# GpSimd adds the last shifted array of VectorE's key tiles, a bank at a time beside VectorE's reads of PSUM

## The chip, the cores and the metric

The kernel runs on one core of a Trainium2 chip. The metric is the device time of one launch in microseconds (us), the median of several runs. A core has TensorE (matmuls, PE in the profile), VectorE (DVE), ScalarE (ACT), GpSimd (POOL) and SyncE (SP, which here only issues DMAs). A profile is one separate execution with the hardware profiler on; its span runs from the first to the last recorded instruction.

## What is computed

An attention block and a gated feed-forward block over the same 2048 rows of 512, mixed by a gate per row. The feed-forward block takes `A_x` too.

```python
def _A_ref(x, wqkv, wo):                       # 32 heads of 16
    q, k, v = ...                              # (x @ wqkv), split by head
    scores = einsum("bhqd,bhkd->bhqk", q, k) * (Dh ** -0.5)
    p = softmax(scores, axis=-1)
    return einsum("bhqk,bhkd->bhqd", p, v)... @ wo

def _B_ref(x, w_gate, w_up, w_down):           # hidden size 1792
    return (silu(x @ w_gate) * (x @ w_up)) @ w_down

g = sigmoid((x * gate_w).sum(-1, keepdims=True))
return g * _A_ref(...) + (1 - g) * _B_ref(...)
```

## The kernel before

**Units and key tiles.** Attention is cut into 32 units: a block of 512 queries by a group of 4 heads. A unit has 16 key tiles of 128 keys, so there are 512 key tiles in all. A key tile has four banks of scores, one for each head: 128 keys by 512 queries in fp32, one PSUM bank each. For every tile TensorE makes the scores, some engine makes exponentials of them, and TensorE multiplies these by V into the unit's accumulator `o_ps` (a "P·V pass": four matmuls, one for each head, in four column strips of the array).

**Two ways to an exponential.** Most tiles go through ScalarE: a score group of two banks (`s_t`) is read by one activation that writes two banks of bf16 to `e_all`. The others go through VectorE, which builds bf16 bit patterns: an eviction of each bank `d_t` (`first`, inside `emit_d`, line 845) multiplies by EXP_A, adds EXP_B and writes uint16 into the tile's array `y` of 4 x 512 columns. Read as bf16 this is a rough exponential. Such a tile is finished in one of two ways:

- four arrays: `copy` (line 887) adds the constants 25, 56 and 94 (`SHIFTS`) to the whole array, each into an array of its own; TensorE does four P·V passes, on `y` and on the three shifted arrays, whose errors cancel out in the sum. This costs VectorE four evictions and three additions of 128 x 2048.
- two arrays: `bits` (line 895) masks the array twice and `product` (line 904) multiplies; TensorE does two P·V passes. VectorE does four evictions, two masks and one product.

`quad` (line 1542) chooses between the two by how much time TensorE has to spare in the plan.

**Arrays.** The arrays (`c_t`, in seven slots, NS; the last slot lies in `kaug` or `wd_t`) are taken by `take_home` and given back by `drop` when their last reader is planned to end. At most three tiles have a live `y` (NY, counted by `y_live`).

**The plan.** The order on every engine is fixed while the kernel is built. A planner keeps clocks for TensorE, ScalarE and VectorE (`plan.pe`, `plan.act`, `plan.dve`) and adds a price in microseconds for each instruction that it emits; `ordered` ties each instruction behind the one before it on its engine. Work for VectorE waits in three lists:

- `owed`: evictions and small steps of projections, the feed-forward block and the normalisation, put there by `later` with a price and the time at which it may start, and emitted by `pay`;
- `d_wait`: evictions of `d_t` (`pay_d`);
- `vops`: the additions, masks and products over whole arrays (`pay_v`).

`fill_dve` (line 924) takes from these by an order of preference as long as VectorE's clock is behind TensorE's. `v_unit` (line 1517) decides whether a further key tile goes to VectorE: it does if VectorE, by its clock and its queued work, can be done before ScalarE ends the tiles it still has. So the share of the two engines follows from the prices. `force` (line 384) emits a chain of work at once when something needs it.

**Feed-forward and projections.** They run as column matmuls between the score groups, paced by deadlines (`Pacer`). Their results are read from PSUM by VectorE and, for the gate's tanh, by ScalarE.

**GpSimd** only fills constants at the start. All DMAs are on SP's and ScalarE's queues.

Of the kernel before, what the change touches and what calls it, by code (L numbers as in the profile page):

```python
# [11 lines left out]
BF16 = mybir.dt.bfloat16  # L12
F32 = mybir.dt.float32
U16 = mybir.dt.uint16
F16 = mybir.dt.float16


# [62 lines left out]
def kernel(  # L80
# [99 lines left out]
            return lambda *a, **kw: ordered(f(*a, **kw))  # L180

    vec = Ordered(nc.vector)
    queue = Ordered(nc.sync)


# [95 lines left out]
    for j in range(4):  # L281
        nc.gpsimd.memset(sel_t[32 * j:32 * j + 1, j:j + 1], 1.0)

    kb = const.tile([P, NB], F32, name="kb")
    gval = const.tile([P, KT], F32, name="gval")
    omg = const.tile([P, KT], F32, name="omg")
# [4 lines left out]


    class Plan:
        pe = dve = act = 0.0
        mode = last = None
        seq = 0
        slot = -1
# [13 lines left out]
    FLIP, UNIT_US = 0.105, 0.217  # L311
    TO_ACT, ACT_FIX, ACT_COL, ACT_IN = 0.485, 0.064, 0.4265, 0.167
    ACT_PE, DVE_PE, PE_DVE, ACT_DVE = 0.055, 0.08, 0.24, 0.06

    def spend(mode, mms, ready=0.0):

# [2 lines left out]
        plan.pe = max(plan.pe + (FLIP if mode != plan.mode else 0.0), ready) + (0.226 if mode == "F" else UNIT_US) * mms  # L319
        plan.mode = mode  # L320

    def later(cost, f, ready=None, key=None):

        c = plan.chain
        if c is not None:
            c.owed += 1
        ready = plan.pe + PE_DVE if ready is None else ready
        owed.insert(sum(o[0] <= ready for o in owed), (ready, cost, f, c, key))

    def spend_v(cost, ready=0.0, key=None):  # L330

        if key is not None and key == plan.last:
            cost += 0.13
        plan.last = key
        plan.dve = max(plan.dve, ready) + cost

    def pay(i=0):
        ready, cost, f, c, key = owed.pop(i)
        spend_v(cost, ready, key)
        keep, plan.chain = plan.chain, None  # L340
        f()
        plan.chain = keep
        if c is not None:
            c.owed -= 1
            if c.done():
                c.done_at = plan.slot
# [35 lines left out]
        return mms  # L382

    def force(c):
        for a in c.after + c.begun:
            force(a)
        while not c.out():
            while c.cond is not None and not c.cond():
                if owed:
                    pay()  # L390
                else:
                    for f in at.pop(min(at)):
                        f()
            emit_piece(c)
        while c.owed:
            pay()
# [135 lines left out]
    def q_pieces(qb, b):  # L532
        def landed(p):
            me = plan.chain
            later(0.6, lambda: end(p, me), key=("q", b))

        def rows(t, r):
            for hh in range(8):
                gg, j = hh // 4, hh % 4
                if (b, gg) != (0, 0):  # L540
                    queue.dma_start(out=get_q(qb, 2 * b + gg)[32 * j + r:32 * j + r + DH, j % 2, :],
                                      in_=t[DH * hh:DH * (hh + 1), :])

        def end(p, me):
            qst = work.tile([P, QBW], BF16, tag="qst", name="qst")
            vec.tensor_copy(out=qst[:, :], in_=p[:, :])
            m_free(p, plan.dve)
            rows(qst, 0)

            aq = work.tile([P, QBW], BF16, tag="aq", name="aq")  # L550

            def mag():
                vec.tensor_scalar(out=aq[:, :].bitcast(U16), in0=qst[:, :].bitcast(U16), scalar1=0x8000, scalar2=None,
                                  op0=ALU.bitwise_or)
                plan.chain = me
                later(0.21, weigh, plan.dve, ("q", b))

            def weigh():
                vec.tensor_scalar(out=aq[:, :], in0=aq[:, :], scalar1=kb[:, b:b + 1], scalar2=None, op0=ALU.mult)
                rows(aq, DH)  # L560
            plan.chain = me
            later(0.21, mag, plan.dve, ("q", b))
        return columns(DC, "qp", lambda dc: wqk[:, dc, P * b:P * (b + 1)],
                       lambda dc: xT[:, dc, qb * QBW:(qb + 1) * QBW], landed)

    def q0_pieces(qb):

        st = {}

        def landed(p):  # L570
            st["p"] = p
            later(0.6, mag, key=("aq", qb))
            later(0.21, clear, key=("aq", qb))

        def mag():
            vec.tensor_copy(out=mt[:, 5, :], in_=st["p"][:, :])

        def clear():
            vec.tensor_scalar(out=mt[:, 5, :].bitcast(U16), in0=mt[:, 5, :].bitcast(U16), scalar1=0x7FFF, scalar2=None,
                              op0=ALU.bitwise_and)  # L580

        def bound():
            bound_add(st["p"], kneg0, mt[:, 5, :])
            spend("C", 1)
            variants(st["p"], q0[qb], work.tile([P, QBW], BF16, tag="qst", name="qst")[:, :])
        return (columns(DC, "qp", lambda dc: wpad[0][:, dc, :], lambda dc: xT[:, dc, qb * QBW:(qb + 1) * QBW], landed),
                [(1, bound, False)])
# [6 lines left out]
    def variants(p, to, q, more=()):  # L594
# [7 lines left out]
                vec.tensor_scalar(out=to[:, v, :], in0=q, scalar1=vsel[:, v:v + 1], scalar2=None, op0=ALU.mult)  # L602
        key = object()
        later(0.6, copy, key=key)
        later(0.4, select, key=key)
        for cost, f in more:
            later(cost, f, key=key)

    def gate_end():
# [3 lines left out]
        def end():  # L613
# [1 line left out]
            vec.reciprocal(gval[:, :], omg[:, :])  # L615
            vec.tensor_tensor(out=omg[:, :], in0=ge[:, :], in1=gval[:, :], op=ALU.mult)
            vec.reciprocal(odds[:, :], ge[:, :])
        later(0.5, end, plan.act + ACT_DVE)

    def turn_odds():  # L620
        rd = work.tile([P, QBW], BF16, tag="rd", name="rd")[:, :].bitcast(F32)
# [223 lines left out]
    def emit_d(i, rows=32):  # L845
# [12 lines left out]
        def first():  # L858
# [4 lines left out]
                              op0=ALU.mult, op1=ALU.add)  # L863
            m_free(d_t, plan.dve)
            cur[0] -= 1
            if cur[0]:
                return
            plan.last = ("y", n)
            if groups[n] == 2:
                vops.extend([(0.6, lambda: bits(n, 0, y), ("y", n), n, True), (0.6, lambda: bits(n, 1, y), None, n, True),  # L870
                             (MUL_US, lambda: product(n, h, y), None, n, False)])
            else:
                users[h][0] = 2
                ready(n, 0, h, y)
                for k in range(1, 4):
                    vops.append((0.6, lambda k=k: copy(n, k, h, y), ("y", n) if k == 1 else None, n, True))
        d_wait.append((plan.pe + UNIT_US + PE_DVE, first, n))

    waiting = {}
    copies = {}  # L880
# [6 lines left out]
    def copy(n, k, i, y):  # L887
        h, c = home()
        vec.tensor_scalar(out=c, in0=y, scalar1=SHIFTS[k - 1], scalar2=None, op0=ALU.add)
        ready(n, k, h, c)  # L890
        if k == 3:
            drop(i, plan.dve + 0.05)
            y_live[0] -= 1

    def bits(n, k, y):
        h, c = home()
# [21 lines left out]

    def pay_v():
        cost, f, key, _, _ = vops.pop(0)  # L920
        spend_v(cost, 0.0, key)
        f()

    def fill_dve():

        while plan.dve <= plan.pe + 0.2:
            now = plan.dve
            due = [k for k, o in enumerate(owed) if o[0] <= now + 0.05]
            free = [k for k in due if owed[k][4] is None or owed[k][4] != plan.last]
            fit = bool(vops) and vops[0][3] // KT <= closed + AHEAD and c_ready() <= now  # L930
            if fit and vops[0][3] // KT < au and vops[0][2] != plan.last:
                pay_v()
            elif d_wait and d_wait[0][2] // KT < au and d_wait[0][0] <= now + 0.05:
                pay_d()
            elif free:
                pay(free[0])
            elif d_wait and d_wait[0][0] <= now + 0.05:
                pay_d()
            elif fit and vops[0][2] != plan.last:
                pay_v()  # L940
# [1 line left out]
                pay(due[0])  # L942
            elif fit:
                pay_v()
            elif d_wait or owed or vops and vops[0][3] // KT <= closed + AHEAD:
                t = min([w[0] for w in d_wait] + [o[0] for o in owed[:1]]
                        + [c_ready()] * bool(vops and vops[0][3] // KT <= closed + AHEAD))
# [108 lines left out]
    def recip(qb, g1, n0):  # L1056
# [9 lines left out]
        def spread():  # L1066
# [8 lines left out]
            for b in range(g1 // 2):  # L1075
                queue.dma_start(out=rb[:, b, :],
                                  in_=rr[8 * b:8 * b + 8, :].unsqueeze(1).broadcast_to([8, DH, QBW]))
        at.setdefault(n0 + 6, []).append(lambda: later(1.1 if full else 0.87, spread))
        for b in range(g1 // 2):
            def norm(b=b):  # L1080
                vec.tensor_tensor(out=onc[qb][:, b, :], in0=onc[qb][:, b, :], in1=rb[:, b, :], op=ALU.mult)
                normed.add((qb, b))
            at.setdefault(n0 + 13 + b, []).append(lambda norm=norm: later(0.345, norm))

    def denominators(p, osb):
        for tq in range(TQ):
# [140 lines left out]
    def bound_all():  # L1227
        def f():
            k_neg(kneg0, 1, kneg1)
            k_neg(kneg0, 2, kneg0)  # L1230
        later(0.8, f)

    def q0_again(p):

# [5 lines left out]
            plan.act += 0.48  # L1240
            ratio_done.append(0)
        variants(p, q0[0], q0_bf[1])
        at.setdefault(8, []).append(lambda: later(0.6, differ))
        at.setdefault(10, []).append(scale)

    def scale_part(p):
# [16 lines left out]
    q_of[0] = again  # L1263

    def gate_column():
        later(0.1, lambda: vec.tensor_copy(out=wv[:, :, 63:64], in_=gw_col[:].unsqueeze(2)))
    gate_w_in = pace.add([(0.2, gate_column, False)], 9, 11, [v_late])
    v_rest = [pace.add(v_pieces(tt), 2, int(14 + 3 * tt), [gate_w_in]) for tt in range(KT)]

# [14 lines left out]
    for qb in range(QB):  # L1284
        for b in range(NB):
            d = UNIT.index((qb, max(2 * b, 1))) * KT
            after = []
            if qb == 0:
# [3 lines left out]
                    ks += prev  # L1292

                def bnd(b=b):
                    later(2.46, lambda: k_bound(b))
                after = prev = [pace.add([(0.2, bnd, False)], 0, d - 34, ks)]

            if b == 0:
# [191 lines left out]
    def next_pv():  # L1490
        flush_act()
        while not pv_list(None):
# [3 lines left out]
                pay_v()  # L1496
            elif owed:
                pay()
            else:
                lone_d()  # L1500
        emit_pv(pv_list(None)[0])
# [15 lines left out]
    def v_unit():  # L1517
# [4 lines left out]
        while vu < UNITS:  # L1522
            if vu > au + 1 or vu in q_of and not (q_of[vu].done() and (vu < QB or plan.slot >= q_of[vu].done_at + 3)):
                return None
            left = hi[vu] - (at_ + begun if vu == au else 0)
            if vu >= au and left > 0 and (vu or hi[0] > KT // 2):
                end = plan.act + (left - 1) * TILE_US + ((hi[au] - at_) * TILE_US if vu > au else 0.0)
                busy = sum(v[0] for v in vops) + 0.6 * (len(owed) + len(d_wait))
# [78 lines left out]
                continue  # L1607
        emit_group(w, ride, rel)
    flush_act()
    while closed < UNITS or vops or vcur:  # L1610
        fill_dve()
        while owed and owed[0][0] <= plan.pe:
            pay()
# [86 lines left out]
```

## Time and profile before

| what | us |
|---|---|
| median of 3 runs | 769.22 (768.71 to 769.77) |
| time of the profiled execution | 768.54 |
| its span | 766.8 |
| weight loads on TensorE (PEld), busy | 246.0 |
| 56 tanh activations of the gate (th), busy | 35.0 |
| 112 feed-forward steps on VectorE (gs and mt), busy | 38.0 + 38.1 |
| 32 + 4 + 3 + 1 products on VectorE, busy | 38.8 + 4.9 + 3.7 + 1.2 |

A line of the groups gives the source line, the engine, the operation, out<-in with shapes, and the count; behind the bar the busy time, the mean duration of one in ns, and the idle time of the engine just before it with what ended it. The kernel's matmuls, activations and VectorE instructions all go through helpers, so lines 168, 171 and 180 stand for all of them, and groups are told apart by the names of their tiles. Three quantities matter here: the busy time of each engine in each stretch of the span, the number of instructions of each kind, and the pitch from one start to the next, since a duration is a latency and neighbours overlap.

### The profile page before, as it was taken

What the parts mean: (1) busy time and instruction counts of PE and PEld (TensorE: products, weight loads), DVE (VectorE), ACT (ScalarE), POOL (GpSimd) and SP (SyncE); (2) the same over time, 40 slices, a digit from 0 to 9 for tenths busy, and PEclk for the clock granted to TensorE, in tenths of its full rate; (3) what the DMA queues carried; (4) which work ended last, traced back from release to release, by engine and by line L of the source; (5) the groups of instructions that cost most, each with busy time, mean ns of one, the idle gap of its engine ahead of it and who ended that gap; (6) DMA issues with size and microseconds to landing.
All of it is one profiled execution on the core that took longest, in us unless ns stands there. A gap on an engine that the chain in (4) does not pass through costs nothing.

```text
span 766.8 us, 24169 instructions
## 1 busy us (share of the span) xinstructions
PE 740.6 (97%) x10109; PEld 246.0 (32%) x10109; DVE 734.6 (96%) x1234; ACT 750.8 (98%) x843; POOL 10.6 (1%) x25
## 2 busy tenths in 40 slices
PE   8999999999999999999999999999999999999997
PEld 3333333333333233333333333323333333333332
DVE  7899999999999999999999999999999999999993
ACT  6999999999999999999999999999999999999996
POOL 5000000000000000000000000000000000000000
PEclk9999999999999999999999999999999999999999
DMA  9000313144210013211200130212000232100001
GB/s 222 6 2 15 67 21 78 34 117 87 62 28 13 17 41 78 58 33 28 51 18 24 32 95 21 69 28 56 12 19 17 69 80 56 31 18 7 22 30 35
DMA packets 91029, 34.53 MB, mean 45 GB/s; under 512 B 75488, under 2 KB 90472, under 8 KB 90920
## 3 DMA queue, kind: packets, MB, share of 16 engines
q1 hardware_dynamic: 89192, 32.66, 17.7%
q8 instruction: 79, 1.29, 0.7%
q10 hardware_dynamic: 1728, 0.33, 0.2%
q14 instruction: 30, 0.25, 0.1%
HBM read 21.55 MB, written 2.35 MB: 31 GB/s over the span
## 4 chain that ended last, share of the span: by engine, by line
ACT 48%; PE 27%; DVE 13%; issue 11%; DMA 0%; DVEq 0%; ACTq 0%
ACT e_all L171 45%; DVE c_t L180 9%; PE s_t L168 9%; PE o_ps L168 8%; PE gu L168 5%; ACT th L171 2%; PE dps L168 2%; DVE kaug L180 1%; PE qp L168 1%; DVE mt L180 1%; PE vp L168 1%; PE warm L168 1%; DVE gs L180 1%; DVE osb L180 1%; PE kp L168 0%
## 5 line engine op out<-in xcount | busy, mean ns | idle before, releaser
L171 ACT ACTIVATE e_all<-s_t 128x1024 bf16<-128x1024 f32 x774 | 722.9, 1049 | 3.2 <-PE s_t L168 1.6
L180 DVE TENSOR_SCALAR c_t<-d_t 128x512 uint16<-128x512 f32 x432 | 285.8, 681 | 4.8 <-PE d_t L168 4.5
L168 PE MATMUL s_t<-qx,kaug 32*128 32x512 bf16 (+1 forms) x1224 | 237.6, 385 | 11.6 <-ACT e_all L171 10.2
L168 PE MATMUL o_ps<-e_all,vaug 128*32 128x512 bf16 (+3 forms) x2024 | 170.1, 334 | 0.8 <-ACT e_all L171 0.6
L168 PEld LDWEIGHTS <-kaug 32*128 32x128 bf16 (+1 forms) x2048 | 80.6, 91 | 275.8 <-issue 268.6
L180 DVE TENSOR_SCALAR c_t<-c_t 128x2048 uint16<-128x2048 uint16 x236 | 157.7, 682 | 0.4
L168 PE MATMUL d_t<-qx,kaug 32*128 32x512 bf16 x408 | 153.2, 384 | 0.3 <-DVE qx L180 0.3
L168 PEld LDWEIGHTS <-vaug 128*32 128x32 bf16 x4112 | 101.9, 95 | 131.8 <-issue 94.7
L168 PE MATMUL o_ps<-c_t,vaug 128*32 128x512 bf16 (+3 forms) x1768 | 136.3, 341 | 0.7 <-DVE osb L180 0.6
L168 PE MATMUL gu<-xT,wg 128*32 128x512 bf16 x896 | 71.9, 383 | 0.1
L168 PE MATMUL gu<-xT,wu 128*32 128x512 bf16 x896 | 70.2, 383 | 0.0
L168 PE MATMUL ops<-wd_t,mt 128*32 128x512 bf16 x672 | 58.1, 382 | 0.0
L180 DVE TENSOR_SCALAR kaug<-d_t 128x512 uint16<-128x512 f32 x60 | 40.0, 682 | 0.9 <-PE d_t L168 0.7
L180 DVE SCALAR_TENSOR_TENSOR mt<-gs,gu 128x512 bf16<-128x512 bf16 x56 | 38.1, 680 | 1.6
L180 DVE TENSOR_TENSOR c_t<-c_t 128x2048 bf16<-128x2048 bf16 x32 | 38.8, 1214 | 0.0
L168 PE MATMUL s_t<-q,kaug 32*128 32x512 bf16 (+1 forms) x188 | 36.4, 385 | 2.4 <-ACT e_all L171 2.2
L180 DVE SCALAR_TENSOR_TENSOR gs<-th,gu 128x512 bf16<-128x512 bf16 x56 | 38.0, 678 | 0.1
L171 ACT ACTIVATE th<-gu 128x512 bf16<-128x512 f32 x56 | 35.0, 624 | 0.0
L168 PEld LDWEIGHTS <-mt 128*32 128x32 bf16 (+1 forms) x1037 | 25.0, 95 | 26.2 <-issue 19.6
L180 DVE TENSOR_SCALAR kaug<-c_t 128x2048 uint16<-128x2048 uint16 x46 | 31.3, 680 | 0.0
L180 DVE TENSOR_SCALAR c_t<-kaug 128x2048 uint16<-128x2048 uint16 x42 | 28.1, 683 | 0.0
L168 PEld LDWEIGHTS <-wg 128*32 128x32 bf16 x896 | 18.1, 94 | 25.3 <-issue 21.3
(142 smaller groups left out, 434.1 us busy)
## 6 DMA issues: line engine op xcount, KB each, us to landing
wg<-in_B_w_gate_dram SPq DMA_DIRECT2D x56, 128.0 KB
wu<-in_B_w_up_dram SPq DMA_DIRECT2D x56, 128.0 KB
on<-osb SPq DMA_DIRECT2D x120, 16.0 KB
rb<-rr SPq DMA_DIRECT2D x15, 128.0 KB
wd_t<-in_B_w_down_dram SPq DMA_DIRECT2D x7, 256.0 KB
qx<-qst SPq DMA_DIRECT2D x96, 16.0 KB
qx<-aq SPq DMA_DIRECT2D x96, 16.0 KB
out_dram<-o_t SPq DMA_DIRECT2D x12, 128.0 KB
```

The costliest lines, as they stand in the source:

```text
L168: return ordered(nc.tensor.matmul(*args, **kw))
L171: ordered(nc.scalar.activation(*args, **kw))
L180: return lambda *a, **kw: ordered(f(*a, **kw))
```

## The change

In a four-array tile the third addition, of 94, is taken from VectorE. GpSimd does it on the array's bits read as 32-bit integers, two columns at once, by adding an array `lift` that holds 94 in both halves. A job (`jobs`) is opened with a tile's first eviction; each eviction adds its bank to the job's list. `lifted` emits a piece of m neighbouring banks. GpSimd gets a clock `plan.pool` with prices of its own.

```diff
+    lift = const.tile([P, 2], U16, name="lift")
+    nc.gpsimd.memset(lift[:], int(SHIFTS[2]))
...
+    GPS = 1
+    OWN = 1
+    POOL_IN, POOL_FIX, POOL_ONE, POOL_PE, POOL_OVER = 0.12, 0.09, 0.45, 0.2, 0.1
...
             cur[0] -= 1
+            if groups[n] == 4 and GPS:
+                if n not in jobs:
+                    jobs[n] = [h, y, None, None, [], 0]
+                jobs[n][4].append(i)
...
-                users[h][0] = 2
+                users[h][0] = 2 + GPS
                 ready(n, 0, h, y)
-                for k in range(1, 4):
+                for k in range(1, 4 - GPS):
                     vops.append((0.6, lambda k=k: copy(n, k, h, y), ("y", n) if k == 1 else None, n, True))
...
+    def lifted(n, m=1, own=False):
...
+        if own:
+            spend_v(0.07 + 0.1335 * m, 0.0, None, True)
+            vec.tensor_scalar(out=c[:, cols], in0=y[:, cols], scalar1=SHIFTS[2], scalar2=None, op0=ALU.add)
+            fast_last[0] = last_of[vec.engine.engine]
+        else:
+            ins = gps.tensor_tensor(out=c[:, cols].bitcast(I32), in0=y[:, cols].bitcast(I32),
+                                    in1=lift[:, :].bitcast(I32).broadcast_to([P, m * QBW // 2]), op=ALU.add)
+            if fast_last[0] is not None:
+                tc.add_manual_dep(ins.ins, fast_last[0].name,
+                                  mybir.DependencyInfo(mybir.DependencyClass.Sync, mybir.DependencyReason.DATA), reason="beside reads of PSUM")
+            plan.pool = max(plan.pool, plan.dve + POOL_IN) + POOL_FIX + POOL_ONE * m
+        end = plan.dve + DVE_PE if own else plan.pool + POOL_PE
...
+    def beside(span):
+
+        if not jobs or plan.pool > plan.dve + 0.05:
+            return
...
+        m = int((span + POOL_OVER - POOL_IN - POOL_FIX) / POOL_ONE)
+        while m > 0 and not any(all(j in left for j in range(i, i + m)) for i in left):
+            m -= 1
+        if m > 0:
+            lifted(n, m)
```

VectorE's work is now of two kinds. Operations that read and write SBUF alone (whole-array additions, masks, products, and the small steps of the normalisation and projections) carry a flag `fast`; in the plan they start no earlier than `plan.pool`. The others read PSUM. The piece on GpSimd gets a semaphore wait for the last `fast` instruction emitted before it (`fast_last`); VectorE gets no wait for GpSimd.

```diff
-        plan.dve = max(plan.dve, ready) + cost
+        plan.dve = max(plan.dve, ready, plan.pool if fast else 0.0) + cost
...
+            slow = [k for k in due if not owed[k][5]]
             fit = bool(vops) and vops[0][3] // KT <= closed + AHEAD and c_ready() <= now
+            d_due = bool(d_wait) and d_wait[0][0] <= now + 0.05
+            if plan.pool > now + 0.1 and (slow or d_due):
+                fit = False
+                due = slow
...
+            urgent = fit and vops[0][3] // KT < au and vops[0][2] != plan.last
+            if not urgent and (d_due or free and not owed[free[0]][5]):
+                beside(span(now))
...
+            elif OWN and plan.pool <= now and own_now(now):
+                pass
```

`fill_dve` calls `beside` just before it emits a read of PSUM. `span` adds up the reads of PSUM that are due one after another from now, and `beside` gives GpSimd as many neighbouring banks as fit into them by the prices, with 0.1 us over. While the plan has GpSimd busy and a read of PSUM is due, `fast` work is held back. If nothing else can start, `own_now` lets VectorE add the banks left over itself, once all four are evicted. Three smaller edits: `force` returns at once for a chain that is done, `v_unit` counts the tile that ScalarE is at as begun in any case, and the loops at the end also wait for open jobs.

## The prediction

> **What bounds the kernel now.** I read the busy shares first, then the stages, then the groups with each shape apart, then the order of work on VectorE and the few instructions of GpSimd.
>
> ```profile
> PE 740.6 (97%) x10109; PEld 246.0 (32%) x10109; DVE 734.6 (96%) x1234; ACT 750.8 (98%) x843; POOL 10.6 (1%) x25
> ...
> ACT 48%; PE 27%; DVE 13%; issue 11%; DMA 0%; DVEq 0%; ACTq 0%
> ```
> Three engines are full at once and the chain of waits changes hands between them; GpSimd does nothing after the start. DMA has no share of the chain. Next the stages: start, two halves of the middle, tail.
>
> ```profile
> 0.00:30.00 30.00, 25.61 (x275) 10.36 (x275) 22.41 (x56) 22.14 (x27) 10.61 (x25) 1.00 0.60 145
> 30.00:400.00 370.00, 361.04 (x4995) 119.63 (x4991) 362.02 (x607) 368.42 (x413) 0.00 (x0) 1.00 0.19 44
> 400.00:745.00 345.00, 336.71 (x4651) 109.94 (x4648) 341.58 (x557) 344.59 (x388) 0.00 (x0) 1.00 0.15 38
> 745.00:766.80 21.80, 17.21 (x199) 6.09 (x195) 8.58 (x17) 15.61 (x18) 0.00 (x0) 0.97 0.10 32
> ```
> The columns are length, then busy time and count of PE, PEld, DVE, ACT, POOL, clock, DMA. In the 715 us from 30 to 745 ScalarE is busy 713.0, VectorE 703.6, TensorE 697.8 (97.6%). Less work on VectorE therefore pays only if the planner turns it into fewer exponentials on ScalarE. What it has to trade stands in the groups:
>
> ```profile
> L171 ACT ACTIVATE e_all<-s_t 128x1024 bf16<-128x1024 f32 x774 | 722.9, 1049 | 3.2 <-PE s_t L168 1.6 <-ACT e_all L171 0.5 <-PE d_t L168 0.4
> ...
> L180 DVE TENSOR_SCALAR c_t<-d_t 128x512 uint16<-128x512 f32 x432 | 285.8, 681 | 4.8 <-PE d_t L168 4.5
> L180 DVE TENSOR_SCALAR c_t<-c_t 128x2048 uint16<-128x2048 uint16 x236 | 157.7, 682 | 0.4
> ...
> L180 DVE TENSOR_TENSOR c_t<-c_t 128x2048 bf16<-128x2048 bf16 x32 | 38.8, 1214 | 0.0
> ```
> 774 exponentials at two per key tile are 387 tiles on ScalarE. VectorE's evictions are 432 here, 60 into kaug and 8 into wd_t: 500, four per tile, 125 tiles. The products (32 + 4 + 3 + 1) make 40 of these two-array tiles, so 85 are four-array tiles. A check: array-to-array additions and masks are 236 + 46 + 42 + 6 + 5 = 335 = 85 x 3 + 40 x 2. The means above are latencies; the pitch is read from the order of work:
>
> ```profile
> 403.79 0.68 DVE L180 TENSOR_SCALAR c_t<-c_t 128x2048 uint16<-128x2048 uint16 x1
> 404.39 1.28 DVE L180 TENSOR_SCALAR c_t<-d_t 128x512 uint16<-128x512 f32 x2
> 405.59 0.68 DVE L180 TENSOR_SCALAR kaug<-c_t 128x2048 uint16<-128x2048 uint16 x1
> 406.23 0.75 DVE L180 TENSOR_SCALAR o_t<-ops,omg 128x512 bf16<-128x512 f32 x1
> ```
> An addition over a whole array begins 0.60 us before the next instruction, and so does an eviction of one bank; each start follows the last with no gap. Counted over the whole order, the 747 reads of PSUM stand in 325 runs between other work: 106 of one, 115 of two, 53 of three, 51 of more.
>
> **The change, part by part.** *Removed from VectorE:* the third addition of each four-array tile, 85 x 0.60 = 51.0 us, 7.2% of its busy time in the middle. The tile falls from seven steps (4.20 us) to six (3.60 us).
>
> *Added to GpSimd:* four one-bank integer additions per tile, 340 banks, in instructions of one to four banks; at the run lengths above (2.3 reads on average, not all with banks ready) I estimate about 200 instructions. No row shows a two-input addition on GpSimd. The nearest:
>
> ```profile
> L521 POOL MEMSET q<- 128x1024 bf16 x1 | 1.0, 952 | 0.0
> ...
> L267 POOL MEMSET vaug<- 128x256 bf16 x1 | 0.3, 315 | 0.0
> L264 POOL TENSOR_SCALAR_AFFINE_SELECT ident<-ident 128x128 bf16<-128x128 bf16 x1 | 0.3, 292 | 0.0
> L1684 POOL MEMSET const-bfloat16-1.0<- 128x1 bf16 x1 | 0.1, 101 | 0.0
> ```
> A bank is 256 integers. Writing alone gives 0.315 us as the low end. The select reads and writes 128 elements in 0.292, of which 0.101 is the fixed part, so 1.49 ns an element: 0.10 + 256 x 1.49 ns = 0.48 us with one input. A second input at the pace of writing ((952 - 101) / 1023 = 0.83 ns) adds 0.21: 0.70 us is the high end. The diff's own constants plan 0.09 + 0.45 = 0.54 and a start 0.12 after VectorE; that lies between the one-input and the two-input price, and I take it.
>
> *Where it lies:* beside a run of k PSUM reads, which cover 0.60 k. The piece ends 0.12 + 0.09 + 0.45 k after the run's start: 0.06 past one read, 0.09 inside two, 0.24 inside three. If the next whole-array operation on VectorE must wait for the piece, only single reads cost: with some 100 of the 200 instructions behind one read, 100 x 0.06 = 6 us. At the low end it is nothing, at 0.70 a one-bank piece overruns by 0.12 + 0.70 - 0.60 = 0.22. Net, VectorE gets 51 - 6 = 45 us.
>
> The Trainium skill (SBUF — State Buffer, Who interferes with whom) says that a VectorE instruction in a two-port mode and any GpSimd instruction exclude each other for a whole instruction, while one that reads PSUM does not take the shared pair. No row here shows the two together, so it stands only beside the condition above. The rule against the change is in its GPSIMD Engine Reference (Elementwise — side-by-side cycle accounting): a two-input addition of 2048 fp32 takes 4497 ns; my estimate from it is 0.56 us a bank in place of 0.45. By it the 200 instructions overrun by 0.17 behind one read and some 0.11 behind more, 28 us in place of 6, and the sum would be 757 + 22 = 779.
>
> *What the planner does with it:* a tile moved from ScalarE frees two exponentials there. Of the 801 ScalarE instructions in the middle 56 are th; with some 0.5 us for each of these the other 745 have a pitch of (713 - 28) / 745 = 0.92, so 1.84 us a tile, against 3.60 on VectorE. Both end together if x (1.84 + 3.60) = 45, x = 8.3 tiles, 15.2 us less.
>
> *TensorE:* a tile moved needs four P·V passes instead of one, and two score groups fewer. A pass of four matmuls occupies some 0.22 us (such steps start at 747.18, 747.41 and 747.63), so +0.65 and -0.43, and fewer changes of mode: about zero. But 698 us of work in 700 instead of 715 is 99.7%. The planner's relief is the two-array tile: 0.43 less on TensorE, 4.73 (four evictions, two masks, a product at pitch 1.13) instead of 3.60 on VectorE. To hold TensorE at 99% takes some 7 such tiles, 8 us of VectorE, 2.7 us of the time. That leaves 12.5.
>
> *The rest:* the flags on queued work, the early return of force, the later test in v_unit and the fallback own_now change only the order; one 128x2 memset adds 0.1 us to GpSimd at the start, hidden under its other memsets. No DMA is moved and SP's queue gets nothing. Each piece waits for VectorE's last whole-array operation; behind it on GpSimd is only the next piece, and the P·V passes of the fourth array on TensorE, in order, wait for the piece. If one is late, the next scores and then ScalarE are late, with nothing between them to hide it.
>
> The span of the profiled execution is 766.8 and its time 768.54, 1.7 more; the median shown is 769.22, 0.7 above that. 766.8 - 12.5 + 1.7 + 0.7 = 756.7: **757 us**, with 750 to 764 as the own range of this case.
>
> **Rivals.**
> 1. *GpSimd is slower than planned, and VectorE stands behind it.* The plan packs VectorE solid, so each unplanned microsecond is added to the end. From 12.5 / 200 = 0.06 us per instruction the gain is gone. With a bank at 0.62, halfway from 0.54 to the high end, it is 0.08 per bank, 340 x 0.08 = 27 us at most, with the slack of longer runs (0.09 behind two, 0.24 behind three) some 20: 777. At 0.70 it is 200 x 0.16 = 32 over the plan: 789. The rate of the Trainium skill's GPSIMD Engine Reference would be this rival. For it: no GpSimd row is faster than one element per 0.83 ns and stream. Against: twice that for 256 elements is 0.43, just the 0.45 planned.
> 2. *TensorE takes the gain.* Its 97.6% includes gaps at changes of mode that can't be filled; VectorE then idles 7% and the time stays at 766 to 769. Against: four of twenty equal slices show it at 99% or more.
> 3. *The arrays run out.* Seven slots (NS), three tiles alive (NY); a fourth array filled over several runs of reads holds its slot and the tile's longer, about 3 us each. With 5 tiles fewer on VectorE ScalarE takes 5 x 1.84 = 9 us more: 778. For it: a four-array tile needs four of seven. Against: 715 / 125 = 5.7 us per tile leaves each slot 40 us.
> 4. *It doesn't do what it says:* the fallback makes the array on VectorE in pieces. By the diff's prices four lone banks are 4 x 0.20 = 0.81 instead of 0.60, at most 85 x 0.21 = 18 us: 785.
>
> **How the numbers follow.** Forecast 0.50; rival 1 0.28; rival 2 0.10; rival 3 0.09; rival 4 0.03. Within 0.2% is 767.7 to 770.8, about what repeated runs can't tell from no change; half of rival 2 falls in it. Faster 0.50 + 0.05 = 0.55, same 0.05, slower 0.40. The range begins at 748: no overrun and TensorE holding nothing back is 17 us, 752, and 4 more if some ten two-array tiles become four-array tiles (1.13 us of VectorE each, a third of it time). It ends at 788, with most of rival 1 inside; the parts beyond have less than 0.2 together.
>
> **What would show it.** Right: some 340 banks of integer additions on POOL, at 0.54 or less each; array-to-array additions on VectorE down to two per four-array tile; exponentials down from 774 to some 760; whole-array operations starting at most 0.1 late after a single read. Wrong by rival 1: idle time on VectorE ahead of whole-array additions, put down to nothing or to POOL, and P·V matmuls waiting for POOL. By rival 2: VectorE idle on PE with as many exponentials. By rival 3: more than 774 exponentials. By rival 4: VectorE additions of 512 columns. The prediction falls if the exponentials drop by ten and the time does not.

## The result, and the profile after

| | median, us | runs | lowest to highest |
|---|---|---|---|
| kernel before | 769.05 | 16 | 768.70 to 769.88 |
| changed kernel | 767.64 | 16 | 767.29 to 768.06 |

The ratio is 0.9981, with a 95% interval of 0.9973 to 0.9988: 1.4 us faster, where 757 was forecast. The sign is right, the size is off by a factor of nine, and the time lies inside the wide range but outside the forecast's own one.

The shares and the chain of waits of the changed kernel:

```profile
PE 739.7 (97%) x10049; PEld 242.3 (32%) x10049; DVE 714.6 (93%) x1174; ACT 749.2 (98%) x841; POOL 176.4 (23%) x280
...
ACT 47%; PE 30%; DVE 11%; issue 10%; DMA 0%; DVEq 0%; POOL 0%; ACTq 0%
```

GpSimd works now, and the chain does not run through it. VectorE has 20.0 us less to do, ScalarE 1.6 us less. By stages (length; busy time and count of PE, PEld, DVE, ACT, POOL; clock; DMA):

```profile
0.00:30.00 30.00, 26.00 (x271) 10.45 (x271) 21.59 (x55) 21.32 (x26) 13.11 (x31) 1.00 0.63 145
30.00:400.00 370.00, 361.49 (x4906) 115.36 (x4902) 345.37 (x569) 368.15 (x414) 83.56 (x129) 1.00 0.19 44
400.00:745.00 345.00, 336.61 (x4720) 111.21 (x4722) 338.04 (x534) 344.72 (x387) 78.54 (x119) 1.00 0.16 38
745.00:766.80 21.80, 15.62 (x162) 5.26 (x154) 9.63 (x19) 15.03 (x18) 1.23 (x2) 1.00 0.09 31
```

In the 715 us of the middle VectorE is busy 683.4 (95.6%), 20.2 less than before; TensorE 698.1 and ScalarE 712.9 are where they were. So VectorE was relieved, and the time freed on it lies idle. The groups of VectorE and ScalarE say what the planner did with it:

```profile
L172 ACT ACTIVATE e_all<-s_t 128x1024 bf16<-128x1024 f32 x772 | 721.5, 1049 | 3.3 <-PE s_t L169 1.9
L181 DVE TENSOR_SCALAR c_t<-d_t 128x512 uint16<-128x512 f32 x424 | 280.6, 683 | 14.7 <-PE d_t L169 13.8
...
L181 DVE TENSOR_SCALAR c_t<-c_t 128x2048 uint16<-128x2048 uint16 x189 | 129.9, 695 | 1.4 <-PE o_ps L169 0.2
```

772 exponentials for 774: one key tile has left ScalarE, not eight. VectorE's idle time ahead of the evictions went from 4.8 to 14.7 us, and almost all of it waits for TensorE's scores. Counted as before, VectorE has 504 evictions, 126 tiles; 55 products, so 55 two-array tiles (40 before) and 71 four-array tiles (85 before). Its additions and masks over whole arrays are 252 in all, 71 x 2 + 55 x 2, as the prediction asked for. GpSimd's own groups:

```profile
L181 POOL TENSOR_TENSOR c_t<-c_t,lift 128x256 int32<-128x256 int32 x152 | 93.1, 615 | 384.8 <-DVE c_t L181 310.2 <-PE d_t L169 30.4 <-DVE gs L181 10.1
...
L181 POOL TENSOR_TENSOR c_t<-c_t,lift 128x512 int32<-128x512 int32 x18 | 18.7, 1040 | 28.1 <-DVE c_t L181 23.7 <-PE d_t L169 1.8 <-DVE wd_t L181 1.4
...
L181 POOL TENSOR_TENSOR kaug<-c_t,lift 128x768 int32<-128x768 int32 x1 | 1.5, 1467 | 1.0 <-DVE c_t L181 1.0
```

One bank takes 0.615 us, two 1.040, three 1.467: 0.43 for each further bank, against 0.45 in the diff. All 254 instructions hold 279 banks; the rest of the 71 x 4 = 284 was added by VectorE itself. A piece beside its read, on VectorE and then on GpSimd:

```profile
401.11 1.22 DVE L181 TENSOR_TENSOR c_t<-c_t 128x2048 bf16<-128x2048 bf16 x1
402.24 0.68 DVE L181 TENSOR_SCALAR kaug<-d_t 128x512 uint16<-128x512 f32 x1
402.84 0.79 DVE L181 TENSOR_SCALAR c_t<-c_t 128x2048 uint16<-128x2048 uint16 x1
403.55 1.88 DVE L181 TENSOR_SCALAR kaug<-d_t 128x512 uint16<-128x512 f32 x3
```
```profile
402.47 0.61 POOL L181 TENSOR_TENSOR c_t<-c_t,lift 128x256 int32<-128x256 int32 x1 [7.09 <-DVE c_t L181]
403.71 1.61 POOL L181 TENSOR_TENSOR c_t<-c_t,lift 128x512 int32<-128x512 int32 x2 [0.63 <-DVE c_t L181]
```

The product ends at 402.33 and the piece starts 0.14 later, inside the single read of PSUM. It ends at 403.08; the addition that started at 402.84 takes 0.79 instead of 0.68, and the next instruction comes 0.71 after it instead of 0.60. Here, behind a single read, the piece costs VectorE some 0.11 us. Over the whole trace only 44 of the 252 whole-array additions and masks and 5 of the 55 products overlap a piece in time. Those 44 last 734 ns in the mean, the other 208 last 685 (682 before), so all of this costs VectorE some 2.5 us.

### The profile page after: what moved, and what is told of

The parts are those of the page before. It is cut to its first block, busy times and chain, and to the rows that moved or that the text cites. A ratio compares the mean times of both kernels' runs of the same rounds, so it can differ in the third digit from the quotient of the medians.

```text
span 766.2 us, 24355 instructions
## 1 busy us (share of the span) xinstructions
PE 739.7 (97%) x10049; PEld 242.3 (32%) x10049; DVE 714.6 (93%) x1174; ACT 749.2 (98%) x841; POOL 176.4 (23%) x280
## 4 chain that ended last, share of the span: by engine, by line
ACT 47%; PE 30%; DVE 11%; issue 10%; DMA 0%; DVEq 0%; POOL 0%; ACTq 0%
ACT e_all L172 46%; PE s_t L169 10%; PE o_ps L169 9%; DVE c_t L181 7%; PE gu L169 5%; PE qp L169 2%; ACT th L172 1%; PE ops L169 1%; DVE kaug L181 1%; PE vp L169 1%; DVE mt L181 1%; PE warm L169 1%; PE d_t L169 1%; DVE gs L181 0%; PE dps L169 0%
## 5 line engine op out<-in xcount | busy, mean ns | idle before, releaser
L181 DVE TENSOR_SCALAR c_t<-d_t 128x512 uint16<-128x512 f32 x424 | 280.6, 683 | 14.7 <-PE d_t L169 13.8
L181 POOL TENSOR_TENSOR c_t<-c_t,lift 128x256 int32<-128x256 int32 (+1 forms) x170 | 111.5, 660 | 412.9 <-DVE c_t L181 333.8
L169 PE MATMUL o_ps<-c_t,vaug 128*32 128x512 bf16 (+3 forms) x1808 | 139.1, 334 | 0.4 <-DVE osb L181 0.2
L169 PEld LDWEIGHTS <-vaug 128*32 128x32 bf16 x4052 | 98.7, 95 | 127.6 <-issue 93.0
L181 DVE TENSOR_SCALAR c_t<-c_t 128x2048 uint16<-128x2048 uint16 x192 | 130.8, 689 | 1.4 <-PE o_ps L169 0.2
L169 PE MATMUL gu<-xT,wu 128*32 128x512 bf16 x896 | 72.0, 383 | 0.2 <-DVE c_t L181 0.2
L181 DVE TENSOR_SCALAR kaug<-d_t 128x512 uint16<-128x512 f32 x80 | 53.1, 684 | 2.7 <-PE d_t L169 2.1
L181 POOL TENSOR_TENSOR kaug<-c_t,lift 128x256 int32<-128x256 int32 (+2 forms) x43 | 28.1, 657 | 84.9 <-DVE c_t L181 83.6
L181 DVE TENSOR_TENSOR c_t<-c_t 128x2048 bf16<-128x2048 bf16 x39 | 47.6, 1220 | 0.0
L181 POOL TENSOR_TENSOR c_t<-kaug,lift 128x256 int32<-128x256 int32 (+1 forms) x41 | 26.3, 646 | 73.1 <-DVE c_t L181 57.5
```

Of the source, the lines that this page charges most:

```text
L169: return ordered(nc.tensor.matmul(*args, **kw))
```

## The experiments

Theory A (the second rival of the prediction): TensorE has no time in which to turn VectorE's relief into key tiles. Rival B (its third): GpSimd finishes the arrays late and holds them long, so the planner can't use the relief. Rival C (its first): GpSimd's pieces block VectorE. Each run is beside runs of the kernel before (769.1 to 769.4).

**The addition made by nobody** (`e1_no_third`). The most that the change could give, with no GpSimd at all.

```diff
-            if groups[n] == 4 and GPS:
...
                 ready(n, 0, h, y)
+                ready(n, 3, h, y)
```

> Leaves out the third shifted addition altogether: neither VectorE nor GpSimd makes it, no array is taken for it, and the fourth P.V pass reads the tile's first array again. This is the most that taking the addition off VectorE could ever give. Theory A (TensorE has no time left to turn VectorE's relief into more key tiles): 760 to 763, three or four tiles fewer on ScalarE, VectorE idle 5% and more, TensorE as full as before. Rival B (VectorE's 51 us are all worth a third of themselves, and GpSimd's lateness is what took them): 750 to 753, eight or nine tiles fewer on ScalarE. Rival C (GpSimd's pieces block VectorE's own instructions): between the two, with VectorE back at 98% busy.

Measured 766.42, ratio 0.9963 (0.9950 to 0.9976): 2.8 us. Four tiles left ScalarE (766 exponentials), as theory A has it, but the time fell even less than its 6 to 9 us. The stage from 30 to 740, of the kernel before and then of this one, and this one's chain of waits:

```profile
30.00:740.00 710.00, 692.94 (x9566) 227.65 (x9563) 698.60 (x1155) 708.01 (x794) 0.00 (x0) 1.00 0.17 42
30.00:740.00 710.00, 696.47 (x9527) 223.61 (x9524) 687.20 (x1116) 706.93 (x793) 0.00 (x0) 1.00 0.18 41
```
```profile
PE 52%; DVE 21%; ACT 20%; issue 5%; DMA 1%; SPq 0%; DVEq 0%; ACTq 0%
```

TensorE is at 98.1% (692.9 of 710 before, 97.6%), VectorE at 96.8%. The chain of waits, which ran through ScalarE for 48% of the span and through TensorE for 27%, now runs through TensorE for 52%. That fits theory A. Rival B's 750 is far off: even free of charge the addition was never worth 15 us.

**TensorE relieved, in the kernel before and in the changed one** (`e2_before_less_up`, `e3_after_less_up`). The edit is the same: three of the four steps of each gate and up product.

```diff
-        return [columns(DC, "gu", ...
+        return [columns(3, "gu", ...
```

> The kernel before, with a quarter of the gate and up products left out (three of the four 128-row steps of each, 112 passes of some 0.22 us, 25 us of TensorE). Theory A: before the change VectorE and TensorE were both full, so relieving TensorE alone gives little, two tiles or 3 to 4 us: 765 to 766. Rival B says the same here; a rival that TensorE alone was the bound would have some 12 us or more: 757 and less.

> The changed kernel with the same quarter of the gate and up products left out. Theory A: VectorE has time, so TensorE's relief is now worth more than in the kernel before: 761 to 763, that is 5 to 6 us under the changed kernel and 3 to 4 under the same cut in the kernel before, with more four-array tiles. Rival B (arrays held too long by GpSimd) and rival C (VectorE blocked by GpSimd): the cut gives no more here than in the kernel before, 764 to 766.

Measured 766.86 (0.9973, 0.9964 to 0.9983) before the change and 763.38 (0.9927, 0.9910 to 0.9944) with it. The first is 0.9 above theory A's 765 to 766, and far from the 757 of a TensorE that alone is the bound. With TensorE relieved, the change is worth 3.5 us instead of 1.4. 129 tiles go to VectorE, where the kernel before with the same products left out has 127; 88 of them have four arrays and 41 have two, where the changed kernel as it is has 71 and 55. So it is TensorE's load in the plan that makes the planner turn to two-array tiles. The time lies between A's 761 to 763, missed by 0.4, and the 764 to 766 of B and C; the gap is nearer to A than to B or C, which had no further gain, but the second kernel has four runs only.

**Both relieved** (`e9_no_third_less_up`): the edits of the first and the second run together.

> Leaves out the third shifted addition altogether, as the first experiment, and a quarter of the gate and up products, as the second. It closes a square: VectorE relieved or not, by TensorE relieved or not. Theory A (each engine's relief is worth more when the other has been relieved): without TensorE's relief VectorE's was worth 2.8 us (769.2 to 766.4); with it, it should be worth 5 to 7, from 766.9 to 760 to 762. A rival by which the two reliefs just add up: 764.0. A rival by which GpSimd is what spoils the changed kernel: far under the changed kernel with the same cut, 763.4.

Measured 762.97 (0.9917, 0.9904 to 0.9931). The square:

| | TensorE as it is | a quarter less gate and up |
|---|---|---|
| before | 769.1 to 769.4 | 766.86 |
| changed kernel | 767.64 | 763.38 |
| no third addition | 766.42 | 762.97 |

With TensorE relieved VectorE's relief is worth 3.9 us, not the 5 to 7 that theory A asked for, and not clearly more than the 2.8 of the plain sum. So TensorE's load costs something, but giving it 25 us more is not enough: this part of A failed. The chain of waits is split there, 36% on TensorE, 33% on ScalarE and 23% on VectorE. What holds besides is that the changed kernel with TensorE relieved is within 0.4 us of the kernel that makes no addition at all.

**TensorE relieved much more** (`e4_after_much_less_up`, `e5_before_much_less_up`): one of the four steps left.

> The changed kernel with three quarters of the gate and up products left out (336 passes, some 75 us of TensorE). Theory A: the time goes on falling until VectorE is full again, 758 to 760. Rivals B and C: it stays where the smaller cut left it, within 1 us.

> The kernel before with three quarters of the gate and up products left out, the partner of the same cut in the changed kernel. Theory A: VectorE is full and nothing more comes than from the smaller cut, 765 to 766. If TensorE alone had been the bound before: below 760.

Measured 778.42 (1.0121, 1.0104 to 1.0138) and 793.56 (1.0316, 1.0295 to 1.0336): both slower than with all the work. Two things went wrong at once, so the runs tell nothing of A, B or C. The waits of the first of the two:

```profile
PEld L169 <- DMA wg<-in_B_w_gate_dram: 17.3, 5, 5.8
PE gu L169 <- DMA wg<-in_B_w_gate_dram: 15.6, 4, 5.3
```

The products run through their weights faster than these are fetched, and TensorE's queue waits for them, the scores behind them too. (The two lines are in the main the same pauses, of the weight load and of the matmul.) And the granted clock is 0.983 and 0.981 in the mean, in place of 1.0; the last section comes back to it.

**The plan's hold left out** (`e6_no_hold`).

```diff
-        plan.dve = max(plan.dve, ready, plan.pool if fast else 0.0) + cost
+        plan.dve = max(plan.dve, ready) + cost
```

> The changed kernel, but in the plan VectorE's whole-array operations no longer start only when GpSimd's piece is over (plan.pool is left out of spend_v's start); GpSimd's pieces still wait for the last such operation. Nothing is left out of the computation. Theory A with the plan's hold as a part of the loss: the order that the planner finds moves three more tiles to VectorE, and VectorE's real waiting for GpSimd stays a few us: 762 to 765. Rival C (GpSimd blocks VectorE, and the hold is what contained it): the unplanned overruns come back as waits, 767 and more.

Measured 766.11 (0.9962, 0.9950 to 0.9975), 129 tiles on VectorE. That is 1.5 us under the changed kernel; the two were not run side by side, and their intervals against the kernel before just touch. It is above theory A's 762 to 765 and below rival C's 767, and it is where the kernel without the addition stands. Its stage from 30 to 740:

```profile
30.00:740.00 710.00, 698.19 (x9596) 226.64 (x9595) 689.65 (x1120) 705.96 (x791) 171.55 (x266) 1.00 0.18 42
```

TensorE is at 98.3%, the highest of these runs, and the chain of waits runs through it for 56%. By the medians about half of what the relief can give is lost in the changed kernel to the order that the planner chose around GpSimd's prices, not to GpSimd itself; with intervals that touch, this is likely rather than shown.

**Four tiles alive** (`e7_four_live`): NY 4 for 3.

> The changed kernel with four key tiles alive at a time in place of three (NY 4). Rival B (first arrays held longer by GpSimd run into the limit): one tile more to VectorE, 765.5 to 766.5. Theory A alone: unchanged, 767 to 768.

Measured 768.28 (0.9988, 0.9980 to 0.9997). The planner did move one tile more (770 exponentials), and the time did not fall. Rival B is not the cause: more live tiles don't help, and the first experiment, in which no third shifted array is taken at all, is only 1.2 us under the changed kernel by the medians, which bounds what late arrays can cost. The number of slots was not varied.

**The semaphore wait left out** (`e8_no_sync`).

```diff
-            if fast_last[0] is not None:
+            if False:
                 tc.add_manual_dep(ins.ins, fast_last[0].name, ...
```

> The changed kernel without the semaphore wait that makes each GpSimd piece wait for VectorE's last whole-array operation; only the waits for data are left, so pieces start wherever their bank is ready. The order on every engine is the same. If the wait protects VectorE from being blocked (the idea of one piece per read of PSUM): whole-array additions on VectorE get longer than 0.69 us in the mean, VectorE's busy time rises by 10 us or more and the time to 769 and above. If the two engines don't exclude each other here: no change, 767 to 768.

Measured 779.20 (1.0127, 1.0114 to 1.0141): 11.6 us over the changed kernel, whose order of instructions it has. VectorE's busy time rose from 714.6 to 729.6. The groups of VectorE, of the changed kernel and then of this one:

```profile
L181 DVE TENSOR_SCALAR c_t<-c_t 128x2048 uint16<-128x2048 uint16 x189 | 129.9, 695 | 1.4 <-PE o_ps L169 0.2
L181 DVE TENSOR_TENSOR c_t<-c_t 128x2048 bf16<-128x2048 bf16 x39 | 47.6, 1220 | 0.0
```
```profile
L181 DVE TENSOR_SCALAR c_t<-c_t 128x2048 uint16<-128x2048 uint16 x189 | 137.1, 733 | 1.3 <-PE o_ps L169 0.3
L181 DVE TENSOR_TENSOR c_t<-c_t 128x2048 bf16<-128x2048 bf16 x39 | 50.7, 1301 | 0.0
```

On GpSimd a bank goes from 0.615 to 0.787 us in the largest group. One place of the same kernel, VectorE first:

```profile
405.79 1.63 DVE L181 TENSOR_TENSOR c_t<-c_t 128x2048 bf16<-128x2048 bf16 x1
407.35 0.68 DVE L181 TENSOR_SCALAR kaug<-d_t 128x512 uint16<-128x512 f32 x1
407.95 0.92 DVE L181 TENSOR_SCALAR c_t<-c_t 128x2048 uint16<-128x2048 uint16 x1
```
```profile
405.50 3.84 POOL L181 TENSOR_TENSOR c_t<-c_t,lift 128x256 int32<-128x256 int32 x3 [9.26 <-PE o_ps L169]
```

The row's three pieces hold one, two and one bank. Elsewhere they take 0.615 + 1.040 + 0.615 = 2.27 us, here 3.84 (0.85, 2.02 and 1.06) beside the end of one addition, the product and the next addition; the product takes 1.63 for 1.22 and the addition 0.92 for 0.68, while the read of PSUM between them keeps its 0.68. The Trainium skill (SBUF — State Buffer, Who interferes with whom) says that a VectorE instruction in a two-port mode and a GpSimd instruction contend, as one with two SBUF inputs does with a GpSimd instruction that reads SBUF, and that whoever comes first blocks the other for its whole instruction. The trace agrees: the times above come out roughly if the pieces, the product and the additions take turns. The reads of PSUM are not touched: in the changed kernel the 174 evictions that run beside a piece for more than 0.3 us last 684 ns in the mean, and those beside none 684 too. The wait is what makes the change pay at all.

**Cheap pieces** (`e10_cheap_piece`).

```diff
-            ins = gps.tensor_tensor(out=c[:, cols].bitcast(I32), in0=y[:, cols].bitcast(I32), ...
+            ins = gps.memset(c[:, cols].bitcast(F32), 1.0019378662109375)
```

> The changed kernel, order and waits as planned, but each GpSimd piece writes a constant to its columns instead of reading the bank and adding: the shifted array's values are left out, and a piece should take 0.32 us in place of 0.61. If GpSimd's pieces hold VectorE up in the changed kernel (rival C), the time falls by several us, 764 and less, and VectorE's whole-array additions get shorter. Theory A: the plan already keeps them apart, and the time stays within 1 us, 767 to 768.

Measured 767.09 (0.9971, 0.9961 to 0.9982). A piece of one bank took 0.31 us, VectorE's largest group of additions 684 ns in place of 695, and the time fell by 0.55 us. Rival C is worth no more than that in the changed kernel.

**A tuned version** (`e11_tuned`): the plan's hold left out, NY 4, SPARE 0.25, LEAD 7.0.

> The changed kernel without the plan's hold on whole-array operations, with four tiles alive (NY 4), SPARE 0.25 and LEAD 7.0. Nothing is left out. The planner puts 130 key tiles on VectorE, the changed kernel 126. Theory A: TensorE limits what comes of it; the tiles are worth some 2/3 of 1.84 us each as in the experiments before, 764 to 766. Rival C: VectorE's unplanned waits for GpSimd eat it, 767 or more.

Measured 767.54 (0.9975, 0.9966 to 0.9985), with 764 exponentials, ten fewer than before. It falls outside theory A's 764 to 766 and where rival C put it, but the whole-array additions and masks last 690 ns in the mean, 694 in the changed kernel, so waits for GpSimd have not grown. By the median four tiles more than the changed kernel bought nothing. A part of that is the clock: the two runs with a granted clock of 0.999 and 1.000 took 765.88 and 766.00 us, the two at 0.995 took 768.52 and 768.11, while the changed kernel's runs all have 0.999 or 1.000. The last section shows what the lower clock is.

**The kernel before with another lead** (`e12_before_lead6`): LEAD 6.0 for 8.0, no GpSimd.

> The kernel before, with no GpSimd, and one number of its planner changed: LEAD 6.0 for 8.0, by which VectorE may take a key tile 2 us later. The planner then puts 126 tiles on VectorE, as many as the changed kernel. If the changed kernel's 1.4 us are just one key tile moved, however it is won: 767 to 768, the same as the changed kernel. If GpSimd's relief has a worth of its own: no faster than before, 769.

Measured 769.30 (0.9998, 0.9990 to 1.0007). It has as many exponentials as the changed kernel (772) and is no faster than before. So the 1.4 us are not just a tile moved; it takes VectorE's relief to keep what the tile gives.

**Where the tiles' time went.** Each span can be split along ScalarE: up to the first exponential, 0.917 us for each exponential but the last (the planner's price; in the traces three quarters of the pitches lie between 0.903 and 0.927), 0.477 for each of the 56 th (26.7 us), what is left over (late starts), and the time from the last exponential's start to the end. The counts are of single profiled runs.

| | exponentials | first at | exponentials x 0.917 | late | end | span |
|---|---|---|---|---|---|---|
| before | 774 | 12.5 | 708.8 | 9.5 | 9.2 | 766.8 |
| changed kernel | 772 | 13.3 | 707.0 | 9.9 | 9.2 | 766.2 |
| before, LEAD 6 | 772 | 13.2 | 707.0 | 12.1 | 9.5 | 768.5 |
| no third addition | 766 | 13.5 | 701.5 | 11.7 | 11.2 | 764.7 |
| no hold | 766 | 13.0 | 701.5 | 12.8 | 10.0 | 764.0 |
| tuned | 764 | 12.9 | 699.7 | 16.2 | 9.6 | 765.1 |
| both relieved | 762 | 13.7 | 697.8 | 13.4 | 9.2 | 760.9 |

The first column of times varies by a microsecond; a part of it is the wait for the first weights (0.73 us before, 1.29 in the changed kernel). The others tell the story: every tile moved takes 1.8 us of exponentials off ScalarE, and some of it comes back as late starts and a longer end: 4.2 of 7.3 us without the third addition, 4.1 of 7.3 without the hold, 3.9 of 11.0 with both engines relieved. In the tuned kernel it is 7.1 of 9.1, and with LEAD 6 more than the 1.8; the clock of these two profiled runs was 0.998 and 0.997, so their late starts hold something of that too. In the kernel before 26 starts are late by more than 0.1 us, 6.2 us in all; in the tuned one 46, 12.8 us. By what ended the wait, 2.7 of the 6.2 us are put down to a score matmul of TensorE, and 9.3 of the 12.8 in the tuned kernel. TensorE worked without a pause in the 2 us ahead of 18 of them before (3.5 us) and of 31 in the tuned kernel (6.8 us); there the scores stood behind other matmuls in TensorE's order.

## Why the prediction was wrong

- **Which engines are full:** right for ScalarE and VectorE, in that the time fell clearly only where exponentials left ScalarE; the run with LEAD 6 shows that this alone is not enough. TensorE's 97.6% was read as work, and it isn't (below).
- **What VectorE loses:** right for a tile (0.60 us), too large in sum. At the pitches of the prediction VectorE's tiles cost 85 x 4.20 + 40 x 4.73 = 546 us before and 71 x 3.60 + 55 x 4.73 = 516 after. Of the 51.0 us taken off, 14 x 1.13 = 15.8 went into tiles that became two-array tiles and 4.7 into the one tile more; some 30 are left, and 20 of these show as less busy time. Of the other 10, longer instructions make 6.6: the 252 whole-array additions and masks last 694 ns in the mean instead of 682, 3.0 us in all, and the other instructions 3.6 us more. The four additions that VectorE makes itself are 0.9. The last 3 fit the pauses, 177 of them in place of 119: an instruction ahead of a pause counts as busy for its 0.68 us and not for its pitch of 0.60.
- **GpSimd's price:** near, but not met. A lone bank takes 0.615 us, between the one-input and the two-input price, where the prediction took 0.54 and called 0.54 or less its sign; each further bank takes 0.43 where it took 0.45. 0.62 is just the price for which the first rival forecast 777. The time did not follow it: pieces meet 49 whole-array operations of VectorE and cost it some 2.5 us, not the 6 of the forecast and not the rival's 20, and VectorE had idle time to put them in. The rate by the Trainium skill (GPSIMD Engine Reference, Elementwise — side-by-side cycle accounting; 0.56 us a bank, an estimate from its figure for fp32) does not hold for this integer addition; 0.43 is measured, and that rival's sum of 779 fell with it.
- **The balance of ScalarE and VectorE, and TensorE's share in it:** this is the step that failed. The prediction turned VectorE's 45 us into 8.3 tiles at 1.84 us each, and took only 2.7 us off for TensorE, on the ground that some 7 further two-array tiles would hold it at 99%. The planner made 15 further two-array tiles and moved one tile; 20 us of VectorE's time lie idle. Both terms were mis-sized, the number of tiles and the worth of one: even without the addition, and without the hold, four tiles moved and gave 2.8 and 3.3 us, 0.7 to 0.8 us a tile, because more than half came back as late exponentials and a longer end. TensorE's load is shown as a part of the cause: with a quarter of gate and up left out four tiles move, 41 two-array tiles are left in place of 55, and the change is worth 3.5 us instead of 1.4. It is not the whole: 25 us of relief, with VectorE relieved too, bring 6 us and not the forecast's 12. Theory A's own expectations came out too large in `e1` and `e9` for the same reason: they priced a moved tile without the late starts. The tuned kernel is the case that the prediction named as its fall: ten exponentials fewer, and 1.6 us.
- **TensorE's busy time, which that step rests on:** it does not say how much room TensorE has. With four P·V passes for a four-array tile, two for a two-array tile and one for a tile of ScalarE, the tiles counted above need 807 passes before and 780 after. At the prediction's 0.22 us a pass some 6 us of work went away, and TensorE's busy time in the stage from 30 to 740 stayed, 692.9 us and 693.2. Nor is 98.3% a ceiling: it is the highest share seen over this stage, but four of twenty equal slices of the kernel before stand at 99% or more, as the prediction says, and most of TensorE's pauses there are waits for ScalarE to free a score group. From 30 to 745, in the kernel before (us, times, longest):

```profile
PE s_t L168 <- ACT e_all L171: 12.9, 35, 1.0
```

- **The hold, which the prediction did not price:** of the 3 us that could be had the changed kernel gets about half. In the plan each whole-array operation waits for GpSimd's clock, and three tiles stay on ScalarE that could have left.
- **The rivals:** the second one, TensorE takes the gain, is what came nearest: 766 to 769 with VectorE idle, though 4.4% and not 7%. Its reason, gaps at changes of mode, is not what the pauses show. Of the first the price came and the time did not, and the cheap pieces refute it; the third is refuted by the first experiment and the fourth live tile, the fourth by the count of pieces: 279 of 284 banks are on GpSimd. (The fourth rival's 785 adds its 18 us to the span of 766.8; added to the time of 769.2 they are 787.)

What stays open: why the planner moves no more than six tiles even with both engines relieved, and what of the late starts is TensorE's order rather than its load. No run here changes that order alone.

## What to carry to other kernels

Where three engines are each at 97% or more, a relief of one is worth what the other two can still take, and a busy share does not say what that is: here TensorE's busy time stayed while 27 passes of its work went away. Before building an offload, run the kernel with the work simply left out: that one run would have said that 51 us off VectorE buy 2.8. Work beside VectorE on GpSimd is nearly free if it starts at a read of PSUM (some 2.5 us for 254 pieces here) and costs both engines dearly if it does not (11.6 us).

## What was not expected of the hardware

With three quarters of the gate and up products left out the granted clock fell to 0.983 and 0.981 in the mean, with TensorE busy 91% of the stage from 30 to 740 in both. The row of the second kernel, in tenths over 40 slices:

```profile
PEclk9999999999999999899999999899999998999899
```

In the traces the clock is halved for 3.4 or 6.8 us at a time. In the first kernel three of four such stretches, from 323.6, 487.5 and 651.3, begin 2 to 4 us after TensorE has come to a stop for weights, for 4.6, 5.1 and 5.3 us; in the second kernel four of five begin so, after stops of 2.8 to 5.6 us. A long stop is not needed. In the tuned kernel's profiled run the clock is halved once, behind a stretch in which TensorE was busy 2.59 of 3.50 us and waited at most 0.68 at a time:

```profile
527.00:530.50 3.50, 2.59 (x28) 0.77 (x20) 2.89 (x6) 3.50 (x5) 1.55 (x3) 1.00 0.16 36
530.60:533.80 3.20, 3.20 (x26) 0.56 (x26) 2.62 (x5) 2.39 (x3) 1.65 (x3) 0.50 0.59 133
```

So most of the stretches at half clock followed a stop of TensorE; how little of a pause is enough was not tried.
